# Keys loaded by partition quadrant, values in 8 KB runs, a ring of cells and a third held value pass in a two-layer decode kernel

## The chip, the cores and the metric

The kernel runs on one core of one Trainium2 chip. The metric is the device time of one execution in microseconds (us). Runs of one kernel agree within about 0.5% before the change and within about 1% after it.

## The reference

Two rounds of attention and feed-forward for eight sequences, one new token each. The same caches serve both rounds.

```python
def _A_ref(x, k_cache, v_cache, wq, wo):          # caches: 8 sequences x 8 heads x 8192 rows x 128, bf16
    q = (x @ wq).reshape(B, Sq, Hq, Dh).transpose(0, 2, 1, 3)        # 32 query heads, 4 per cache head
    scores = einsum("bhqd,bhkd->bhqk", q, repeat(k_cache)) * Dh ** -0.5
    o = einsum("bhqk,bhkd->bhqd", softmax(scores), repeat(v_cache))
    return o.transpose(0, 2, 1, 3).reshape(B, Sq, Hq * Dh) @ wo
x = x + _A_ref(layernorm(x), K, V, wq, wo);  x = x + silu_ffn(layernorm(x), w1, w2)
x = x + _A_ref(layernorm(x), K, V, wq, wo);  x = x + silu_ffn(layernorm(x), w1, w2)
```

One head of one sequence has 2 MiB of keys and 2 MiB of values. The kernel reads the keys once (134 MB) and keeps them transposed on the chip between the rounds; it reads the values twice (268 MB). With the weights that makes 482 MB.

## The kernel before

A small planner simulates the kernel when it is built: each load and each computation is a node with an estimated duration. The simulation decides the order in which instructions are written to the queues. Loads go in order through one queue (SP) into a ring of 11 buffers of 512 KB, and a load is issued when a buffer comes free. The parts that the change touches, shortened:

```python
N_GRAN = 11; N_DEF = 2; T_TURN = 1.2              # buffers; value passes held back; planned us of a transpose

def load_v(b, g, P):                              # 4 loads of 512 KB: 128 partitions x 4 KB
    src = A_v_cache[b, g].rearrange("(P n r) d -> P n (r d)", P=4, n=128)
    return load_gran(f"v{b}.{g}.{P}", src[P], 1)

def load_k(b, g, c4):                             # 4 loads of 512 KB: 128 partitions x 4 KB
    src = A_k_cache[b, g].rearrange("(p c4 cg) d -> c4 p (cg d)", p=128, c4=4)
    return load_gran(f"k{b}.{g}.{c4}", src[c4], 1)
# ... (cut)
def turns(b, g):                                  # 32 x 32 blocks of 4-byte words, written 4 words apart
    new = slot(g).bitcast(U32).rearrange("p (k i c4) -> p c4 k i", i=32, c4=4)
    for c4 in range(4):
        kn = load_k(b, g, c4)
        def turn(kn=kn, c4=c4):
            raw = gran(kn.give).bitcast(U32).rearrange("p (k j) -> p k j", j=32)
            op(dve, lambda: dve.transpose(new[:, c4], raw), reads=[res("ring", kn.give)], writes=[res("kt", g)], add=(c4 > 0))
# ... (cut) score matmuls read 128 neighbouring words of the transposed keys as weights; column n of the
# scores becomes partition n of the values, so the row order of keys and values must match
for b in range(-1, NB):                           # sequence b's second round beside b+1's first
    if b >= 0:
        n = ffn_nodes(f"c{b}", prio, b, 1, [x2_node(b, prio)])
        ready = norm_nodes(f"c{b}.ln2", prio, b, 1, [n])
        for h in held:                            # value passes of the sequence before, held back
            values(h)                             # so that the loads go on while ready is computed
    # ... (cut)
            if g % 4 == 0:                        # query weights, 4 x 512 KB into the ring
                second_q.update(queries(f"c{b}", count[0] - 3, g // 4, b, 1, [ready]))
```

Of the kernel before, what the change touches and what calls it, by code (L numbers as in the profile page):

```python
# [11 lines left out]
N_GRAN = 11  # L12
N_SC = 3
N_P = 3
N_DEF = 2
N_OT = 2
N_BD = 4
T_TURN = 1.2
# [94 lines left out]
class Node:  # L113


    __slots__ = ("eng", "dur", "emit", "prio", "deps", "outs", "left", "ready", "end", "take", "give", "name")

    def __init__(self, name, eng, dur, emit, prio, deps):
# [11 lines left out]
        self.give = None  # L130


class Plan:
# [3 lines left out]
    RATE = 2.47  # L137
# [12 lines left out]
    def load(self, name, mib, emit, pool, deps=()):  # L150
        n = Node(name, "DMA", mib * self.RATE, emit, 0, deps)
        n.take = pool
        self.nodes.append(n)
        self.loads.append(n)
        return n

    def run(self, pools):
# [5 lines left out]
        free = {}  # L163
# [10 lines left out]
        waiting = {p: list(b) for p, b in pools.items()}  # L174
# [5 lines left out]
        while True:  # L180
            moved = True
            while moved:
                moved = False
                if li < len(loads):
                    n = loads[li]
                    if n.left == 0 and (n.take is None or waiting[n.take]):
                        buf = waiting[n.take].pop(0) if n.take is not None else None
                        if n.take is not None:
                            n.give = buf
# [23 lines left out]
            elif what == "done":  # L213
                done += 1
                n.end = now
                if n.eng != "DMA" and n.give is not None:
                    for pool, src in n.give:
                        waiting[pool].append(src.give)
# [16 lines left out]
def _build(ctx, nc, A_x, A_k_cache, A_v_cache, A_wq, A_wo, B_w1, B_w2, out):  # L235
# [21 lines left out]
    ring = sb([128, N_GRAN * GR], BF16, "ring")  # L257
# [34 lines left out]
    rsem = [DmaCounter(syn.new_sem(f"ring{i}")) for i in range(N_GRAN)]  # L292
# [16 lines left out]
    def dma(eng, out_ap, in_ap, counter, reads=(), writes=()):  # L309
        syn.acquire(eng, reads, writes)  # L310
        tok = counter.next_tok()
        eng.dma_start(out_ap, in_ap).then_inc(counter.sem, 16)  # L312
        syn.release(tok, reads, writes)

# [13 lines left out]
    def gran(i):  # L328
        return ring[:, i * GR:(i + 1) * GR]
# [8 lines left out]
    def load_gran(name, src, k):  # L338

        n = plan.load(name, 0.5, None, "ring")  # L340

        def emit():
            i = n.give
            dst = gran(i) if k == 1 else gran(i).rearrange("p (k x) -> p k x", k=k)
            dma(sp, dst, src, rsem[i], writes=[res("ring", i)])
# [4 lines left out]
    def load_v(b, g, P):  # L350
        return load_gran(f"v{b}.{g}.{P}", v_src(b, g)[P], 1)

    def v_src(b, g):
        return A_v_cache[b, g].rearrange("(P n r) d -> P n (r d)", P=4, n=128)

    def load_k(b, g, c4):
        src = A_k_cache[b, g].rearrange("(p c4 cg) d -> c4 p (cg d)", p=128, c4=4)
        return load_gran(f"k{b}.{g}.{c4}", src[c4], 1)

    def load_wq(half, kt):  # L360
        return load_gran(f"wq{half}.{kt}", wq_v[:, kt, GR * half:GR * (half + 1)], 1)

    def load_wo(g):
        return load_gran(f"wo{g}", A_wo.rearrange("(g p j) d -> g p (j d)", g=G, j=R)[g], 1)

    def frees(n, pool, src):
        n.give = (n.give or []) + [(pool, src)]
# [7 lines left out]
    def norm_nodes(tag, prio, b0, nb, deps):  # L375
# [54 lines left out]
        m = plan.add(f"{tag}.mean", "DVE", 0.12, mean, prio, [a])  # L430
        v = plan.add(f"{tag}.var", "DVE", 0.3, vari, prio, [m])
        r = plan.add(f"{tag}.root", "POOL", 0.6, root, prio, [v])
        return plan.add(f"{tag}.xn", "DVE", 0.15, apply, prio, [r])


    def ffn_nodes(tag, prio, b0, nb, deps):
# [40 lines left out]
        u = plan.add(f"{tag}.up", "PE", 2.2, up, prio, [n] + ffn_deps)  # L477
        t = plan.add(f"{tag}.tanh", "ACT", 0.3, tanh, prio, [u])
        g = plan.add(f"{tag}.gate", "DVE", 0.15, gate, prio, [t])
        d = plan.add(f"{tag}.down", "PE", 2.2, down, prio, [g])  # L480
        return plan.add(f"{tag}.resid", "DVE", 0.15, resid, prio, [d])


    xr = gran(N_GRAN - 1)[0:NB, 0:D]
    xnr = gran(N_GRAN - 1)[0:NB, D:2 * D]
# [489 lines left out]
```

## Time and profile before

| | before |
|---|---|
| time | 1243.9 us (1242.73 to 1243.91, 3 runs) |
| moved | 484.8 MB, 389 GB/s on average, 408 GB/s on the plateau |
| busy | DVE 57%, PE 51%, the loads' queue 98.7% |

These are lines of the page of the kernel before. The long row has the GB/s of each fortieth of the span. The row of a queue gives packets, MB and the share of the 16 engines' span. A row of part 5 gives the line, engine, operation, output and input, count, busy us and mean ns, and the idle time before it with its releaser. The last two give the count, the KB of a load and its us from issue to landing.

```profile
PE 631.6 (51%) x20640; PEld 593.0 (48%) x20640; DVE 708.4 (57%) x1236; ACT 63.0 (5%) x202; POOL 117.0 (9%) x295
...
GB/s 362 407 398 408 337 371 408 408 408 356 393 408 408 407 371 407 407 408 399 376 409 407 407 394 373 408 408 408 371 389 408 407 407 364 410 407 408 394 339 208
DMA packets 136865, 484.80 MB, mean 389 GB/s; under 512 B 14544, under 2 KB 20448, under 8 KB 136672
...
q1 hardware_dynamic: 136672, 481.90, 98.7%
...
DMA 41%; DVE 25%; issue 20%; PE 10%; SPq 2%; POOL 2%; ACT 0%; POOLq 0%; DVEq 0%
DMA ring<-in_A_k_cache_dram 24%; DVE kts L605 19%; DMA ring<-in_A_v_cache_dram 10%; DMA ring<-in_A_wq_dram 7%; PE sc L656 5%; PE ot L733 2%; SPq L312 2%; DVE sc L678 2%; DVE small L668 2%; PE misc L563 1%; POOL small L673 1%; DVE small L687 1%; POOL small L692 1%; DVE bd L640 0%; PE yt L784 0%
...
L605 DVE STREAM_TRANSPOSE kts<-ring 128x1024 uint32<-128x1024 uint32 x256 | 503.2, 1988 | 116.6 <-DMA ring<-in_A_k_cache_dram 116.4
...
ring<-in_A_v_cache_dram SPq DMA_DIRECT2D x512, 512.0 KB, 10.8
ring<-in_A_k_cache_dram SPq DMA_DIRECT2D x256, 512.0 KB, 10.6
```

The plateau of 408 GB/s fills most slices, and every few slices there is one at 337 to 376: once for each sequence. DVE and PE are busy for half of the time, so the loads bound the kernel. The dips are where compute holds the loads up. The table of windows over one of them shows the columns time, busy us and count of each engine, granted clock, share of the DMA engines, and GB/s:

```profile
core 0: us, PE busy (x) PEld busy (x) DVE busy (x) ACT busy (x) POOL busy (x), PEclk, DMA share, GB/s
270.00:280.00 10.00, 5.06 (x173) 4.76 (x170) 1.44 (x8) 0.18 (x1) 0.56 (x1) 1.00 1.02 406
...
290.00:300.00 10.00, 7.36 (x253) 6.96 (x250) 6.83 (x11) 0.38 (x1) 1.07 (x3) 1.00 0.92 340
300.00:310.00 10.00, 2.70 (x84) 2.47 (x84) 6.18 (x13) 0.77 (x2) 1.34 (x4) 1.00 0.98 380
310.00:320.00 10.00, 6.51 (x229) 6.37 (x230) 5.72 (x10) 0.56 (x2) 0.80 (x2) 1.00 0.94 338
320.00:330.00 10.00, 3.08 (x89) 2.67 (x86) 7.87 (x8) 0.56 (x2) 0.80 (x2) 1.00 1.02 408
```

The waits of the load queue from 270 to 345 us, as engine and line, what was waited for, total us, times, longest us:

```profile
SPq L89 <- DVE kts L605: 19.1, 6, 7.3
SPq L89 <- PE misc L563: 11.2, 2, 6.0
```

The queue waited there for buffers whose keys were not yet transposed and for buffers with query weights.

### The profile page before, as it was taken

The page shows a single profiled execution, that of the slowest core. Times are in us where ns is not written, and L with a number is a line of the kernel's source. Part 1 is how long each engine was busy: PE and PEld are TensorE (multiplying, and loading weights), DVE is VectorE, ACT ScalarE, POOL GpSimd, SP SyncE. Part 2 cuts the span into 40 slices and gives each one's busy share as a digit, 9 for nine tenths or more (in the row PEclk, how much of TensorE's full clock was granted, in tenths as well). Part 3 has the DMA queues.
Part 4 walks back from the last instruction along what each step waited for, and adds up shares of the span by engine and source line. Part 5 has one row for each costly group of instructions (what it writes and reads, how often), then busy time and mean ns, then how long its engine had stood idle before and what let it go on. Part 6 is the DMA issues. An engine that isn't in the chain of part 4 may idle for free.

```text
span 1245.3 us, 45478 instructions
## 1 busy us (share of the span) xinstructions
PE 631.6 (51%) x20640; PEld 593.0 (48%) x20640; DVE 708.4 (57%) x1236; ACT 63.0 (5%) x202; POOL 117.0 (9%) x295
## 2 busy tenths in 40 slices
PE   2334545455554654546454554555555455454555
PEld 2333545445543544545444454544545455444554
DVE  7745466826477265764557546574556826577221
ACT  0000000000000000000000000000000000000000
POOL 1000010101010010110000100110101101011010
DMA  9999999999999999999999999999999999999995
GB/s 362 407 398 408 337 371 408 408 408 356 393 408 408 407 371 407 407 408 399 376 409 407 407 394 373 408 408 408 371 389 408 407 407 364 410 407 408 394 339 208
DMA packets 136865, 484.80 MB, mean 389 GB/s; under 512 B 14544, under 2 KB 20448, under 8 KB 136672
## 3 DMA queue, kind: packets, MB, share of 16 engines
q1 hardware_dynamic: 136672, 481.90, 98.7%
q8 instruction: 162, 2.65, 0.9%
q14 instruction: 31, 0.25, 0.1%
HBM read 481.83 MB, written 0.01 MB: 387 GB/s over the span
## 4 chain that ended last, share of the span: by engine, by line
DMA 41%; DVE 25%; issue 20%; PE 10%; SPq 2%; POOL 2%; ACT 0%; POOLq 0%; DVEq 0%
DMA ring<-in_A_k_cache_dram 24%; DVE kts L605 19%; DMA ring<-in_A_v_cache_dram 10%; DMA ring<-in_A_wq_dram 7%; PE sc L656 5%; PE ot L733 2%; SPq L312 2%; DVE sc L678 2%; DVE small L668 2%; PE misc L563 1%; POOL small L673 1%; DVE small L687 1%; POOL small L692 1%; DVE bd L640 0%; PE yt L784 0%
## 5 line engine op out<-in xcount | busy, mean ns | idle before, releaser
L605 DVE STREAM_TRANSPOSE kts<-ring 128x1024 uint32<-128x1024 uint32 x256 | 503.2, 1988 | 116.6 <-DMA ring<-in_A_k_cache_dram 116.4
L733 PE MATMUL ot<-p,ring 128*128 128x4 bf16 x8192 | 287.4, 167 | 177.0 <-DMA ring<-in_A_v_cache_dram 115.7
L656 PE MATMUL sc<-bd,kts 128*128 128x16 bf16 x8192 | 278.2, 174 | 160.7 <-issue 53.2
L733 PEld LDWEIGHTS ot<-p,ring 128*128 128x128 bf16 x8192 | 255.5, 104 | 193.6 <-DMA ring<-in_A_v_cache_dram 131.1
L656 PEld LDWEIGHTS sc<-bd,kts 128*128 128x128 bf16 x8192 | 249.8, 104 | 168.9 <-issue 56.0
L673 POOL PARTITION_ALL_REDUCE small<-small x128 | 48.1, 376 | 728.9 <-DVE small L668 631.8
L668 DVE TENSOR_REDUCE small<-sc 128x4 f32<-128x256 f32 x128 | 51.9, 406 | 107.6 <-PE sc L656 107.4
L683 ACT ACTIVATE p<-sc 128x256 bf16<-128x256 f32 x128 | 49.0, 383 | 729.6 <-DVE sc L678 729.6
L784 PE MATMUL yt<-z,ring 128*128 128x4 bf16 x1024 | 36.8, 166 | 93.1 <-DVE z L762 89.8
L692 POOL PARTITION_ALL_REDUCE small<-small x128 | 55.0, 431 | 268.4 <-DVE small L687 266.1
L784 PEld LDWEIGHTS yt<-z,ring 128*128 128x128 bf16 x1024 | 33.0, 104 | 96.2 <-issue 96.0
L563 PE MATMUL misc<-xn,ring 128*128 128x1 bf16 (+1 forms) x1152 | 36.2, 166 | 68.7 <-DMA ring<-in_A_wq_dram 62.1
L563 PEld LDWEIGHTS misc<-xn,ring 128*128 128x128 bf16 x1152 | 33.8, 104 | 71.1 <-issue 64.9
L678 DVE TENSOR_TENSOR sc<-sc,small 128x256 f32<-128x256 f32 x128 | 57.1, 447 | 18.2 <-POOL small L673 17.9
L687 DVE TENSOR_REDUCE small<-p 128x4 f32<-128x256 bf16 x128 | 51.2, 401 | 21.3 <-ACT p L683 21.0
L632 PE MATMUL qx<-qab,sel 128*128 128x4 bf16 x256 | 16.6, 169 | 54.5 <-DVE bd L640 54.5
L696 DVE RECIPROCAL small<-small 128x4 f32<-128x4 f32 x128 | 21.6, 168 | 34.6 <-POOL small L692 34.6
L632 PEld LDWEIGHTS qx<-qab,sel 128*128 128x128 bf16 x256 | 11.8, 106 | 56.5 <-DVE bd L640 56.5
L640 DVE TENSOR_TENSOR bd<-qx,mask 128x64 bf16<-128x64 f32 x128 | 27.7, 217 | 16.2 <-PE qx L632 16.0
L571 DVE CAST qtb<-misc 128x4 bf16<-128x4 f32 (+1 forms) x32 | 5.3, 166 | 54.3 <-PE misc L563 54.3
L743 DVE TENSOR_TENSOR qab<-ot,small 128x4 bf16<-128x4 f32 x64 | 10.0, 157 | 43.6 <-PE ot L733 43.4
L762 DVE TENSOR_TENSOR z<-ot,small 128x16 bf16<-128x16 f32 x64 | 10.5, 164 | 37.7 <-PE ot L755 37.7
(61 smaller groups left out, 206.3 us busy)
## 6 DMA issues: line engine op xcount, KB each, us to landing
ring<-in_A_v_cache_dram SPq DMA_DIRECT2D x512, 512.0 KB, 10.8
ring<-in_A_k_cache_dram SPq DMA_DIRECT2D x256, 512.0 KB, 10.6
ring<-in_A_wq_dram SPq DMA_DIRECT2D x72, 512.0 KB, 10.8
ring<-in_A_wo_dram SPq DMA_DIRECT2D x64, 512.0 KB, 11.0
kts<-in_A_wo_dram SPq DMA_DIRECT2D x2, 2048.0 KB, 16.9
w<-in_B_w_dram SPq DMA_DIRECT2D x2, 1792.0 KB, 14.9
ring<-in_A_x_dram SPq DMA_DIRECT2D x1, 8.0 KB
out_dram<-ring SPq DMA_DIRECT2D x1, 8.0 KB
```

The source lines that it names most:

```text
L563: steps.append(lambda h=h, kt=kt, c=c: pe.matmul(qp[:, h * nb:(h + 1) * nb], gran(wn[kt].give)[:, c:c + DH], xn[:, b0:b0 + nb, kt], start= ...
L605: op(dve, lambda: dve.transpose(new[:, c4], raw), reads=[res("ring", kn.give)], writes=[res("kt", g)], add=(c4 > 0))
L632: steps.append(lambda fe=fe: pe.matmul(QX[:, R * fe:R * fe + R], sel[:, fe].rearrange("p a j -> p (a j)"), qsrc, start=True, stop=True))
L656: steps.append(lambda cg=cg, fe=fe: pe.matmul(sc[:, 16 * cg:16 * cg + 16], kv[:, cg, fe // 2, fe % 2], bd[:, 16 * fe:16 * fe + 16], start= ...
L668: op(dve, lambda: dve.tensor_reduce(mxp[sm], sv.rearrange("p (k h) -> p h k", h=R), AX.X, ALU.max), reads=[res(*scr)], writes=[res("mxp", ...
L673: op(pool, lambda: pool.partition_all_reduce(mxa[sm], mxp[sm], 128, bass.bass_isa.ReduceOp.max), reads=[res("mxp", sm)], writes=[res("mxa" ...
L678: op(dve, lambda: dve.tensor_tensor(v, v, mxa[sm].unsqueeze(1).to_broadcast([128, NCH, R]), ALU.subtract), reads=[res("mxa", sm)], writes= ...
L683: op(act, lambda: act.activation(pt[:, :], sv, ACT.Exp, scale=SM_SCALE), reads=[res(*scr)], writes=[res("p", sm)])
L687: op(dve, lambda: dve.tensor_reduce(ssm[sm], pt[:, :].rearrange("p (k h) -> p h k", h=R), AX.X, ALU.add), reads=[res("p", sm)], writes=[re ...
L692: op(pool, lambda: pool.partition_all_reduce(ssa[sm], ssm[sm], 128, bass.bass_isa.ReduceOp.add), reads=[res("ssm", sm)], writes=[res("ssa" ...
L733: steps.append(lambda cg=cg, k=k: pe.matmul(ot[:, 0:R], vt[:, cg, :], pt[:, k:k + R], start=(P == 0 and cg == 0), stop=(P == 3 and cg == N ...
L784: steps.append(lambda j=j, dt=dt: pe.matmul(YT[:, dt * R:(dt + 1) * R], w[:, j, dt * 128:(dt + 1) * 128], zt[:, R * j:R * j + R], start=(g ...
```

## The change

The intent: a transpose that writes neighbouring words should be faster than one that writes a word every 16 bytes. For that the 128 columns of a score block must be (c4, i) instead of (i, c4), and then a value row order exists in which each partition reads 8 KB in one run. The price is that the keys' partitions, (quadrant, i), no longer lie at one stride in the cache. So each 1 MiB half of a head's keys is loaded by four transfers, one for each quadrant of 32 partitions. The ring is cut into cells of 512 KB and keys and values take two neighbouring ones. Three value passes instead of two are held back, and the first query weights come behind the first of them. The planner's durations are revised.

```diff
-N_GRAN = 11
+N_CELL = 11
-N_DEF = 2
+N_DEF = 3
-T_TURN = 1.2
+T_TURN = 1.07
@@ planner: loads take 1 or 2 neighbouring cells (cut) @@
+    def load_cells(name, cells, parts):
+        n = plan.load(name, cells, None)
+        def emit():
+            buf = gran(n.give, cells)
+            for k, (dst, src) in enumerate(parts):
+                dma(sp, dst(buf), src, rsem[n.give], writes=cells_of(n) if k == 0 else (),
+                    adds=cells_of(n) if k else ())
@@ values and keys @@
+    def load_v(b, g, half):
+        src = A_v_cache[b, g].rearrange("(n hh y) d -> hh n (y d)", n=128, hh=2)
+        return load_cells(f"v{b}.{g}.{half}", 2, [(lambda buf: buf, src[half])])
+    def load_k(b, g, half):
+        src = A_k_cache[b, g].rearrange("(c4 i P x) d -> P i c4 (x d)", c4=4, i=32, P=4)
+        return load_cells(f"k{b}.{g}.{half}", 2, [
+            (lambda buf, P=P: buf[32 * P:32 * P + 32, :].rearrange("p (c4 x) -> p c4 x", c4=2),
+             src[P, :, 2 * half:2 * half + 2, :]) for P in range(4)])
@@ transposes @@
-        new = slot(g).bitcast(U32).rearrange("p (k i c4) -> p c4 k i", i=32, c4=4)
+        new = slot(g).bitcast(U32).rearrange("p (k c4 i) -> p c4 k i", i=32, c4=4)
@@ held passes @@
-            for h in held:
+            for k, h in enumerate(held):
+                if k == 1:
+                    second_q.update(queries(f"c{b}", prio, 0, b, 1, [ready]))
                 values(h)
-                    if g % 4 == 0:
+                    if g % 4 == 0 and g >= (4 if held else 0):
@@ revised planner durations of matmuls and small operations (cut) @@
```

More of the change, by code (lines that the diff above doesn't have):

```diff
@@ L113 @@
 class Node:
-    __slots__ = ("eng", "dur", "emit", "prio", "deps", "outs", "left", "ready", "end", "take", "give", "name")
+    __slots__ = ("eng", "dur", "emit", "prio", "deps", "outs", "left", "ready", "end", "take", "give", "name", "cells")
     def __init__(self, name, eng, dur, emit, prio, deps):
@@ L130, in __init__ @@
         self.give = None
+        self.cells = 0
 class Plan:
-    RATE = 2.47
+    RATE = {1: 2.57, 2: 2.51}
     LAND = 2.0
@@ L148, in add, with load @@
         return n
-    def load(self, name, mib, emit, pool, deps=()):
-        n = Node(name, "DMA", mib * self.RATE, emit, 0, deps)
-        n.take = pool
+    def load(self, name, cells, emit, deps=(), ring=True):
+        n = Node(name, "DMA", cells * 0.5 * self.RATE.get(cells, 2.57), emit, 0, deps)
+        n.take = ring
+        n.cells = cells
         self.nodes.append(n)
@@ L155, in load, with place, run @@
         return n
-    def run(self, pools):
+    @staticmethod
+    def place(free, cells):
+        if cells == 1:
+            alone = [c for c in free if c - 1 not in free and c + 1 not in free]
+            return min(alone or free, default=None)
+        starts = [c for c in free if c + 1 in free]
+        return min(starts, default=None)
+    def run(self, cells):
         for n in self.nodes:
@@ L173, in run @@
         wire = 0.0
-        waiting = {p: list(b) for p, b in pools.items()}
+        idle = set(cells)
         for n in self.nodes:
@@ L185, in run @@
                     n = loads[li]
-                    if n.left == 0 and (n.take is None or waiting[n.take]):
-                        buf = waiting[n.take].pop(0) if n.take is not None else None
-                        if n.take is not None:
-                            n.give = buf
+                    at = self.place(idle, n.cells) if n.take else None
+                    if n.left == 0 and (at is not None or not n.take):
+                        if n.take:
+                            n.give = at
+                            idle -= set(range(at, at + n.cells))
                         order.append((now, seq, n))
@@ L216, in run @@
                 if n.eng != "DMA" and n.give is not None:
-                    for pool, src in n.give:
-                        waiting[pool].append(src.give)
+                    for src in n.give:
+                        idle |= set(range(src.give, src.give + src.cells))
                 for o in n.outs:
@@ L255, in bank @@
         return ctx.enter_context(nc.psum_tensor(name, [128, 512], FP32))
-    ring = sb([128, N_GRAN * GR], BF16, "ring")
+    ring = sb([128, N_CELL * GR], BF16, "ring")
     kts = sb([128, G * SLOT], BF16, "kts")
@@ L291, in _build @@
     ksem = [DmaCounter(syn.new_sem(f"kt{i}")) for i in range(2)]
-    rsem = [DmaCounter(syn.new_sem(f"ring{i}")) for i in range(N_GRAN)]
+    rsem = [DmaCounter(syn.new_sem(f"ring{i}")) for i in range(N_CELL)]
     wsem = {n: DmaCounter(syn.new_sem(f"w_{n}")) for n in ("w1", "w2", "x")}
@@ L307, in op, with dma @@
         syn.release(tok, reads, writes, add=add)
-    def dma(eng, out_ap, in_ap, counter, reads=(), writes=()):
+    def dma(eng, out_ap, in_ap, counter, reads=(), writes=(), adds=()):
         syn.acquire(eng, reads, writes)
@@ L313, in dma @@
         syn.release(tok, reads, writes)
+        syn.release(tok, (), adds)
     def mms(steps, reads=(), writes=(), add=False):
@@ L326, in _build, with gran, cells_of @@
     wo_v = A_wo.rearrange("(h p) d -> p h d", p=128)
-    def gran(i):
-        return ring[:, i * GR:(i + 1) * GR]
+    def gran(i, cells=1):
+        return ring[:, i * GR:(i + cells) * GR]
+    def cells_of(n):
+        return [res("ring", n.give + k) for k in range(n.cells)]
     def slot(i, n=1):
@@ L335, in _build, with frees @@
     scored = {}
-    def load_gran(name, src, k):
-        n = plan.load(name, 0.5, None, "ring")
+    def load_cells(name, cells, parts):
+        n = plan.load(name, cells, None)
         def emit():
-            i = n.give
-            dst = gran(i) if k == 1 else gran(i).rearrange("p (k x) -> p k x", k=k)
-            dma(sp, dst, src, rsem[i], writes=[res("ring", i)])
+            buf = gran(n.give, cells)
+            for k, (dst, src) in enumerate(parts):
+                dma(sp, dst(buf), src, rsem[n.give], writes=cells_of(n) if k == 0 else (),
+                    adds=cells_of(n) if k else ())
         n.emit = emit
         return n
-    def load_v(b, g, P):
-        return load_gran(f"v{b}.{g}.{P}", v_src(b, g)[P], 1)
-    def v_src(b, g):
-        return A_v_cache[b, g].rearrange("(P n r) d -> P n (r d)", P=4, n=128)
-    def load_k(b, g, c4):
-        src = A_k_cache[b, g].rearrange("(p c4 cg) d -> c4 p (cg d)", p=128, c4=4)
-        return load_gran(f"k{b}.{g}.{c4}", src[c4], 1)
+    def load_v(b, g, half):
[6 more added lines that the diff above has]
+             src[P, :, 2 * half:2 * half + 2, :]) for P in range(4)])
     def load_wq(half, kt):
-        return load_gran(f"wq{half}.{kt}", wq_v[:, kt, GR * half:GR * (half + 1)], 1)
+        return load_cells(f"wq{half}.{kt}", 1, [(lambda buf: buf, wq_v[:, kt, GR * half:GR * (half + 1)])])
     def load_wo(g):
-        return load_gran(f"wo{g}", A_wo.rearrange("(g p j) d -> g p (j d)", g=G, j=R)[g], 1)
-    def frees(n, pool, src):
-        n.give = (n.give or []) + [(pool, src)]
+        return load_cells(f"wo{g}", 1, [
+            (lambda buf: buf, A_wo.rearrange("(g p j) d -> g p (j d)", g=G, j=R)[g])])
+    def frees(n, src):
+        n.give = (n.give or []) + [src]
     tail = gran(1)
@@ L429, in norm_nodes @@
         a = plan.add(f"{tag}.stats", "PE", 0.3 + 0.2 * nb, stats, prio, deps)
-        m = plan.add(f"{tag}.mean", "DVE", 0.12, mean, prio, [a])
-        v = plan.add(f"{tag}.var", "DVE", 0.3, vari, prio, [m])
+        m = plan.add(f"{tag}.mean", "DVE", 0.18, mean, prio, [a])
+        v = plan.add(f"{tag}.var", "DVE", 0.45, vari, prio, [m])
         r = plan.add(f"{tag}.root", "POOL", 0.6, root, prio, [v])
-        return plan.add(f"{tag}.xn", "DVE", 0.15, apply, prio, [r])
+        return plan.add(f"{tag}.xn", "DVE", 0.3, apply, prio, [r])
     def ffn_nodes(tag, prio, b0, nb, deps):
@@ L476, in ffn_nodes @@
         n = norm_nodes(tag + ".ln", prio, b0, nb, deps)
-        u = plan.add(f"{tag}.up", "PE", 2.2, up, prio, [n] + ffn_deps)
-        t = plan.add(f"{tag}.tanh", "ACT", 0.3, tanh, prio, [u])
-        g = plan.add(f"{tag}.gate", "DVE", 0.15, gate, prio, [t])
-        d = plan.add(f"{tag}.down", "PE", 2.2, down, prio, [g])
-        return plan.add(f"{tag}.resid", "DVE", 0.15, resid, prio, [d])
-    xr = gran(N_GRAN - 1)[0:NB, 0:D]
-    xnr = gran(N_GRAN - 1)[0:NB, D:2 * D]
+        u = plan.add(f"{tag}.up", "PE", 1.65, up, prio, [n] + ffn_deps)
+        t = plan.add(f"{tag}.tanh", "ACT", 0.2, tanh, prio, [u])
+        g = plan.add(f"{tag}.gate", "DVE", 0.18, gate, prio, [t])
+        d = plan.add(f"{tag}.down", "PE", 1.65, down, prio, [g])
+        return plan.add(f"{tag}.resid", "DVE", 0.18, resid, prio, [d])
+    xr = gran(N_CELL - 1)[0:NB, 0:D]
+    xnr = gran(N_CELL - 1)[0:NB, D:2 * D]
     st6 = negm[0:NB, 0:6]
     mv = var[0:NB, 0:2]
-    last = res("ring", N_GRAN - 1)
+    last = res("ring", N_CELL - 1)
     def consts():
@@ L508, in _build @@
     c_n = plan.add("consts", "POOL", 1.5, consts, -10)
-    x_n = plan.load("x", 0.05, lambda: dma(sp, xr, x_in, wsem["x"], writes=[last]), None)
+    x_n = plan.load("x", 1, lambda: dma(sp, xr, x_in, wsem["x"], writes=[last]), ring=False)
     def first_norm():
@@ L545, in _build @@
     f5 = plan.add("f.copy", "DVE", 0.4, first_copy, -5, [f4])
-    frees(f4, "ring", x_n)
-    x_n.give = N_GRAN - 1
+    frees(f4, x_n)
+    x_n.give = N_CELL - 1
     def queries(tag, prio, half, b0, nb, deps):
@@ L565, in mul @@
                             start=(kt == 0), stop=(kt == KT - 1)))
-                mms(steps, reads=[res("ring", w.give) for w in wn] + [res("xn")], writes=[res("misc")])
+                mms(steps, reads=[r for w in wn for r in cells_of(w)] + [res("xn")], writes=[res("misc")])
             def copy(g0=g0, g1=g1, qp=qp):
@@ L575, in copy @@
                        reads=[res("misc")], writes=[res("qab", g) for g in range(g0, g1)])
-            m = plan.add(f"{tag}.q{g0}", "PE", 0.65 * (g1 - g0), mul, prio, wn + deps + last)
+            m = plan.add(f"{tag}.q{g0}", "PE", 0.5 * (g1 - g0), mul, prio, wn + deps + last)
             last = [plan.add(f"{tag}.qc{g0}", "DVE", 0.17, copy, prio, [m])]
@@ L581, in queries @@
         for w in wn:
-            frees(m, "ring", w)
+            frees(m, w)
         return out_n
@@ L598, in turns, with turn @@
         tn = []
-        new = slot(g).bitcast(U32).rearrange("p (k i c4) -> p c4 k i", i=32, c4=4)
-        for c4 in range(4):
-            kn = load_k(b, g, c4)
-            def turn(kn=kn, c4=c4):
-                raw = gran(kn.give).bitcast(U32).rearrange("p (k j) -> p k j", j=32)
-                op(dve, lambda: dve.transpose(new[:, c4], raw), reads=[res("ring", kn.give)],
-                   writes=[res("kt", g)], add=(c4 > 0))
-            n = plan.add(f"t{b}.{g}.{c4}", "DVE", T_TURN, turn, count[0] + 0.5, [kn] + scored.get(g, []) + tn[-1:])
-            frees(n, "ring", kn)
-            tn.append(n)
+        new = slot(g).bitcast(U32).rearrange("p (k c4 i) -> p c4 k i", i=32, c4=4)
+        for half in range(2):
+            kn = load_k(b, g, half)
+            for c in range(2):
+                def turn(kn=kn, c=c, c4=2 * half + c):
+                    raw = gran(kn.give, 2).bitcast(U32).rearrange("p (c k j) -> p c k j", c=2, j=32)
+                    op(dve, lambda: dve.transpose(new[:, c4], raw[:, c]), reads=cells_of(kn),
+                       writes=[res("kt", g)], add=(c4 > 0))
+                tn.append(plan.add(f"t{b}.{g}.{2 * half + c}", "DVE", T_TURN, turn, count[0] + 0.5,
+                                   [kn] + scored.get(g, []) + tn[-1:]))
+            frees(tn[-1], kn)
         kept[b, g] = tn
@@ L659, in score @@
                 mms(steps, reads=[res("kt", g), res("bd", u % N_BD)], writes=[res(*scr)], add=(q > 0))
-            sn.append(plan.add(f"s{u}.{q}", "PE", 0.75, score, pr - 1,
+            sn.append(plan.add(f"s{u}.{q}", "PE", 0.56, score, pr - 1,
                                [tn[3], bn] + ([old[1]] if old else []) + sn[-1:]))
@@ L723, in values @@
         for P in range(4):
-            if P == 3 and wo is not None:
+            if P == 2 and wo is not None:
                 h["wo"] = load_wo(wo)
-            vn = load_v(b, g, P)
+            if P % 2 == 0:
+                vn = load_v(b, g, P // 2)
             def pv(P=P, vn=vn):
-                vt = gran(vn.give).rearrange("p (cg d) -> p cg d", cg=NCG)
+                vt = gran(vn.give, 2).rearrange("p (a cg d) -> p a cg d", a=2, cg=NCG)[:, P % 2]
                 steps = []
@@ L735, in pv @@
                         start=(P == 0 and cg == 0), stop=(P == 3 and cg == NCG - 1)))
-                mms(steps, reads=[res("ring", vn.give), res("p", sm)], writes=[res("ot", o)], add=(P > 0))
-            n = plan.add(f"v{u}.{P}", "PE", 0.65, pv, pr, [h["exp"], vn, old] + vs[-1:])
-            frees(n, "ring", vn)
+                mms(steps, reads=cells_of(vn) + [res("p", sm)], writes=[res("ot", o)], add=(P > 0))
+            n = plan.add(f"v{u}.{P}", "PE", 0.56, pv, pr, [h["exp"], vn, old] + vs[-1:])
+            if P % 2:
+                frees(n, vn)
             vs.append(n)
@@ L787, in mul @@
                         skip_group_check=True))
-            mms(steps, reads=[res("ring", wn.give), res("z", o)], writes=[res("yt")], add=g > 0)
-        n = plan.add(f"w{h['u']}", "PE", 0.65, mul, count[0] - 3, [h["n"], wn, prev])
-        frees(n, "ring", wn)
+            mms(steps, reads=cells_of(wn) + [res("z", o)], writes=[res("yt")], add=g > 0)
+        n = plan.add(f"w{h['u']}", "PE", 0.56, mul, count[0] - 3, [h["n"], wn, prev])
+        frees(n, wn)
         return n
@@ L808, in mul @@
                 writes=[res("yt")], add=g > 0)
-        return plan.add(f"e.w{g}", "PE", 0.65, mul, count[0] - 3, [h["n"], wn, prev])
+        return plan.add(f"e.w{g}", "PE", 0.56, mul, count[0] - 3, [h["n"], wn, prev])
     free_yt = [None]
@@ L821, in load_ffn @@
     def load_ffn():
-        ffn_deps.append(plan.load("w1", 1.75, lambda: dma(
-            sp, w1_sb[:, :, :], B_w1.rearrange("(kt p) f -> p kt f", p=128), wsem["w1"], writes=[res("w1")]), None))
-        ffn_deps.append(plan.load("w2", 1.75, lambda: dma(
-            sp, w2_sb[:, :, :], B_w2.rearrange("(ft p) d -> p ft d", p=128), wsem["w2"], writes=[res("w2")]), None))
+        ffn_deps.append(plan.load("w1", 3.5, lambda: dma(
+            sp, w1_sb[:, :, :], B_w1.rearrange("(kt p) f -> p kt f", p=128), wsem["w1"], writes=[res("w1")]), ring=False))
+        ffn_deps.append(plan.load("w2", 3.5, lambda: dma(
+            sp, w2_sb[:, :, :], B_w2.rearrange("(ft p) d -> p ft d", p=128), wsem["w2"], writes=[res("w2")]), ring=False))
     def x2_node(b, prio):
@@ L838, in load_wo_all @@
         for i in range(2):
-            n = plan.load(f"woall{i}", 2.0, None, None, scored[2 * i])
+            n = plan.load(f"woall{i}", 4, None, scored[2 * i], ring=False)
             def emit(i=i):
@@ L934, in _build @@
     n = plan.add("e.copy", "DVE", 0.5, e_copy, big, [n])
-    order = plan.run({"ring": list(range(N_GRAN - 1))})
+    order = plan.run(range(N_CELL - 1))
     with nc.Block() as block:
```

## The prediction

> **What bounds the kernel now.** Loading. The page counts 484.8 MB in 1245.3 us (389 GB/s), while DVE is busy 57% and PE 51%. The 40 slices show a plateau of 408 GB/s: at that rate the bytes alone take 484.8/408 = 1188 us. The other 57 us are slices below the plateau: about 4 us at the start, about 21 us in the last two slices (the last 15 us move 12 GB/s), and about 32 us in one dip per batch. In a table of 10 us windows the first dip (130 to 170 us) runs at 263, 338, 358, 341 GB/s, the next (280 to 320 us) at 363, 340, 380, 338. There the DMA queue waits for buffers: the queue's own waits there name transposes (19.1 us) and query projections (11.2 us). DVE works through 1.99 us transposes that delay the softmax and normalization steps behind which the held values and query weights sit.
>
> **What changes, costed.**
> 1. Transposes: 256 x 1988 ns (groups by line), for 1024 elements written at a 16-byte stride. [...] DVE is not the bound, so this pays only by shortening the dips.
> 2. Values: 512 loads of 512 KB become 256 of 1 MiB in 8 KB runs. Two rates of this trace give the price of a packet: while the second feed-forward weight lands (1 KB runs) 350 GB/s, that is 46.8 ns per packet and engine; 4 KB runs at 408, 160.6 ns. A line through both (an estimate) gives 8 KB in 312 ns, or 419 GB/s: 268 MB gain about 17 us. This is on the bound.
> 3. A third held pass, and the first query weights loaded after the first held pass: 5 us more of loads that need no result of the feed-forward chain. With point 1, I expect 15 to 22 of the 32 us of dips to go.
> 4. Ring: the same 11 cells, but 1 MiB units are freed later; costs a few us.
> 5. Keys: 256 loads over 128 partitions become 512 of 256 KB over 32 partitions each. Issues on SP cost 0.45 us (timeline, first four), so 1.8 us per MiB against 2.6 us of transfer: hidden.
>
> **Main risk.** [...] Nothing in this trace tests it: every large load there spans 128 partitions. The rest of the change only makes sense if the keys keep their rate, so I hold this less likely than not, at about one in four.
>
> **Predicted:** 1207 us (-3%), range 1180 to 1290. Faster by over 2%: 0.63; within 2%: 0.13; slower: 0.24.
>
> **What would show it.** [...] packets down by some 32,000; slices of values alone at 415 to 420 GB/s; dips once per batch shallower, above 380 GB/s; start and tail as before; windows with key loads as fast as those with values. If wrong: [...] the plateau stays at 408 (then about 1222 us); or dips remain because 1 MiB cells come free too late.

The forecast's sum stands at 1207 us: 1243.9 us before, less about 17 (point 2) and 15 to 22 (point 3), plus a few (point 4). The terms of the main risk said how slow the keys would be if a transfer to 32 partitions were slower than one to 128. They made a second sum, some 1490 us in all. Nothing measured stood behind them then; m1 below measures the rate.

## The result, and the profile after

The changed kernel takes 1686.26 us (1674.02 to 1690.83, 4 runs) against 1243.91 us in the same rounds: 1.354 times as long, 95% interval 1.347 to 1.362. A ratio here is the mean time of one kernel's fast runs over that of the other's of the same rounds, so it is not quite the ratio of the medians quoted beside it.

The lines of the page after that answer to those above:

```profile
PE 630.1 (37%) x20640; PEld 591.2 (35%) x20640; DVE 548.0 (32%) x1236; ACT 62.2 (4%) x202; POOL 117.4 (7%) x295
...
GB/s 258 302 296 268 239 316 275 253 333 304 310 248 231 319 294 313 252 230 321 321 314 279 253 309 312 301 260 302 340 301 278 247 325 290 288 262 239 303 368 242
DMA packets 104094, 484.78 MB, mean 287 GB/s; under 512 B 14544, under 2 KB 20448, under 8 KB 71136
...
q1 hardware_dynamic: 103904, 481.90, 95.4%
...
DMA 71%; issue 9%; DVE 7%; PE 7%; SPq 5%; POOL 1%; ACT 0%; POOLq 0%; DVEq 0%
DMA ring<-in_A_k_cache_dram 36%; DMA ring<-in_A_v_cache_dram 33%; DVE kts L626 5%; SPq L326 5%; PE ot L755 3%; DMA ring<-in_A_wq_dram 1%; PE sc L677 1%; PE misc L584 1%; PE misc L468 1%; PE misc L486 1%; POOL rstd L434 0%; POOL small L694 0%; DVE sc L699 0%; PE yt L807 0%; DVE small L689 0%
...
L626 DVE STREAM_TRANSPOSE kts<-ring 128x1024 uint32<-128x1024 uint32 x256 | 310.8, 1230 | 252.1 <-DMA ring<-in_A_k_cache_dram 252.0
...
ring<-in_A_v_cache_dram SPq DMA_DIRECT2D x256, 1024.0 KB, 15.2
ring<-in_A_k_cache_dram SPq DMA_DIRECT2D x512, 256.0 KB, 10.3
```

The bytes are the same, but the average fell from 389 to 287 GB/s and no slice reaches even 370. The queue's packets still fill 95.4% of the engines' time. The transposes fell from 1988 to 1230 ns and DVE's busy time from 708 to 548 us, and the packets from 136,865 to 104,094, as the change intended. In the chain that ended last, loads rose from 41% to 71% and DVE fell from 25% to 7%. The table of windows near the start, with the columns as above, shows two rates:

```profile
4.00:6.00 2.00, 0.37 (x8) 0.29 (x8) 0.40 (x1) 0.00 (x0) 0.78 (x4) 1.00 1.04 229
6.00:8.00 2.00, 0.00 (x0) 0.00 (x0) 0.00 (x0) 0.00 (x0) 0.00 (x0) 1.00 1.06 229
8.00:10.00 2.00, 0.00 (x0) 0.00 (x0) 1.60 (x4) 0.00 (x0) 0.00 (x0) 1.00 1.01 215
...
14.00:16.00 2.00, 0.00 (x0) 0.00 (x0) 1.46 (x2) 0.00 (x0) 0.00 (x0) 1.00 0.99 395
...
18.00:20.00 2.00, 0.85 (x26) 0.80 (x27) 0.19 (x1) 0.00 (x0) 0.00 (x0) 1.00 1.06 221
```

From 4 to 10 us only keys are under way, and 215 to 229 GB/s arrive at a full DMA share. At 14 us the query weights have their turn, over 128 partitions, and 395 arrive; at 18 us keys again, and 221. (The first packet of values starts at 26 us.)

### The profile page after: what moved, and what is told of

Same layout as the page of the kernel before. It is cut to its first block, busy times and chain, and to the rows that moved or that the text cites. A ratio compares the mean times of both kernels' runs of the same rounds, so it can differ in the third digit from the quotient of the medians.

```text
span 1686.8 us, 44976 instructions
## 1 busy us (share of the span) xinstructions
PE 630.1 (37%) x20640; PEld 591.2 (35%) x20640; DVE 548.0 (32%) x1236; ACT 62.2 (4%) x202; POOL 117.4 (7%) x295
## 2 busy tenths in 40 slices
DMA packets 104094, 484.78 MB, mean 287 GB/s; under 512 B 14544, under 2 KB 20448, under 8 KB 71136
## 3 DMA queue, kind: packets, MB, share of 16 engines
q1 hardware_dynamic: 103904, 481.90, 95.4%
## 4 chain that ended last, share of the span: by engine, by line
DMA 71%; issue 9%; DVE 7%; PE 7%; SPq 5%; POOL 1%; ACT 0%; POOLq 0%; DVEq 0%
DMA ring<-in_A_k_cache_dram 36%; DMA ring<-in_A_v_cache_dram 33%; DVE kts L626 5%; SPq L326 5%; PE ot L755 3%; DMA ring<-in_A_wq_dram 1%; PE sc L677 1%; PE misc L584 1%; PE misc L468 1%; PE misc L486 1%; POOL rstd L434 0%; POOL small L694 0%; DVE sc L699 0%; PE yt L807 0%; DVE small L689 0%
## 5 line engine op out<-in xcount | busy, mean ns | idle before, releaser
L626 DVE STREAM_TRANSPOSE kts<-ring 128x1024 uint32<-128x1024 uint32 x256 | 310.8, 1230 | 252.1 <-DMA ring<-in_A_k_cache_dram 252.0
L677 PE MATMUL sc<-bd,kts 128*128 128x16 bf16 x8192 | 274.7, 174 | 254.9 <-DVE kts L626 223.4
L766 DVE TENSOR_TENSOR qab<-ot,small 128x4 bf16<-128x4 f32 x64 | 10.1, 158 | 88.5 <-PE ot L755 88.4
L653 PE MATMUL qx<-qtb,sel 128*128 128x4 bf16 x256 | 16.6, 168 | 33.8 <-DVE bd L661 32.4
L653 PEld LDWEIGHTS qx<-qtb,sel 128*128 128x128 bf16 x256 | 11.9, 105 | 37.1 <-DVE bd L661 33.2
L653 PE MATMUL qx<-qab,sel 128*128 128x4 bf16 x256 | 16.6, 168 | 21.7 <-DVE bd L661 16.3
```

The lines of the kernel that those rows point to most:

```text
L626: op(dve, lambda: dve.transpose(new[:, c4], raw[:, c]), reads=cells_of(kn), writes=[res("kt", g)], add=(c4 > 0))
L677: steps.append(lambda cg=cg, fe=fe: pe.matmul(sc[:, 16 * cg:16 * cg + 16], kv[:, cg, fe // 2, fe % 2], bd[:, 16 * fe:16 * fe + 16], start= ...
```

## The experiments

Rival theories at the start. **A (partitions):** which partitions a transfer touches sets its rate, so the keys by quadrant run at about half rate (215 to 229 GB/s against 395 for the weights over 128 partitions, in the windows above). **B (small transfers):** 512 transfers of 256 KB instead of 256 of 512 KB cost the time. **C (ring):** cells of 1 MiB come free too late, or the third held pass starves the queue. The expectations also gave a reason for A, a mechanism that no run here shows. What A forecast by that reason alone stands as the author's guess beside what was measured.

One caution holds for every run below that is called correct: four kernels that pair keys with the wrong value rows (e1, e1b, e2, e6) passed the comparison with the reference. I take it that the softmax is nearly flat for these inputs (argued, not tested). So that comparison does not vouch for a row order; where a layout matters I say which one it is.

### m1: the shapes alone

Eight phases of key loads with no compute, drained between phases; the output is wrong.

```python
phases = [("wide 8 KB", wide(4096)), ("wide 4 KB", wide(2048)), ("four wide 2 KB", four_wide),
          ("quadrants 0 1 2 3", quads((0, 1, 2, 3))), ("quadrants 0 2 1 3", quads((0, 2, 1, 3))),
          ("partitions 0 to 63", half(0)), ("partitions 32 to 95", half(32)),
          ("quadrants, two queues", quads((0, 2, 1, 3), act))]
```

> Loads alone, no compute; the output is wrong on purpose. Eight phases of 8 MiB from the key cache, each drained before the next: (1) 128 partitions x 8 KB, (2) 128 x 2 runs of 4 KB, (3) four loads of 256 KB over 128 partitions in 2 KB runs, (4) quadrants 0 1 2 3, four loads of 256 KB over 32 partitions, as in the changed kernel, (5) the same in the order 0 2 1 3, (6) 4 MiB over partitions 0 to 63, (7) 4 MiB over partitions 32 to 95, (8) quadrants with every other load from the ACT queue. Theory A [...]: 1 about 419 GB/s, 2 about 408, 3 about 385, 4 about 222, 5 about 222 or somewhat more, 6 about 222, 7 about 408, 8 above 300. Rival B (a load of 256 KB, or one of few partitions, is slow as such): 3 also near 222 and 7 no better than 6.

One window inside each of the eight phases, in that order; the last two columns are the DMA share and GB/s (before them stand the length, an idle engine and the clock):

```profile
core 0: us, POOL busy (x), PEclk, DMA share, GB/s
5.00:20.00 15.00, 0.00 (x0) 1.00 1.02 427
28.00:44.00 16.00, 0.00 (x0) 1.00 1.03 413
55.00:69.00 14.00, 0.00 (x0) 1.00 1.05 390
75.00:107.00 32.00, 0.00 (x0) 1.00 1.04 223
116.00:146.00 30.00, 0.00 (x0) 1.00 1.04 236
152.00:168.00 16.00, 0.00 (x0) 1.00 1.04 206
178.00:182.00 4.00, 0.00 (x0) 1.00 1.02 382
192.00:212.00 20.00, 0.00 (x0) 1.00 1.04 300
```

The quadrants run at 223 GB/s against 413 for the same 4 KB runs over 128 partitions. Small transfers as such are not slow: 256 KB over 128 partitions run at 390. What decides is which partitions: 64 of them starting at 0 get 206 GB/s, 64 starting at 32 get 382, though that phase is so short (4 MiB) that its window is 4 us. The order 0 2 1 3 shows 236 against 223, which is 6% more, and quadrants split over two queues reach 300. B falls. Why the partitions matter is not shown; theory A holds here as these measured rates.

### e1: wide keys in the changed kernel

```diff
-        src = A_k_cache[b, g].rearrange("(c4 i P x) d -> P i c4 (x d)", c4=4, i=32, P=4)
-        return load_cells(f"k{b}.{g}.{half}", 2, [
-            (lambda buf, P=P: buf[32 * P:32 * P + 32, :].rearrange("p (c4 x) -> p c4 x", c4=2),
-             src[P, :, 2 * half:2 * half + 2, :]) for P in range(4)])
+        src = A_k_cache[b, g].rearrange("(c4 p x) d -> p c4 (x d)", c4=4, p=128)
+        return load_cells(f"k{b}.{g}.{half}", 2, [
+            (lambda buf: buf.rearrange("p (c4 x) -> p c4 x", c4=2), src[:, 2 * half:2 * half + 2, :])])
```

> The changed kernel, with each key half loaded by one transfer over 128 partitions, still 2 runs of 4 KB in each partition, so the same bytes and packets; keys land in other partitions, so the output is wrong on purpose. Everything else of the change stays: unit stride, 8 KB value runs, cells, three held passes. Theory A [...]: the keys run at 408 GB/s again, about 1205 us. Rival C (the ring of 1 MiB units or the third held pass starves the queue): above 1500 us.

Measured: 1221.07 us (4 runs) against 1243.29; ratio 0.982 (0.980 to 0.984). The row order is wrong, so this is no replacement for the kernel. From its page:

```profile
GB/s 364 413 401 415 300 415 413 414 390 416 413 409 414 390 416 411 401 416 395 406 395 416 416 390 413 399 413 394 414 415 412 414 392 416 411 407 416 380 384 201
...
q1 hardware_dynamic: 97760, 481.87, 97.9%
...
L625 DVE STREAM_TRANSPOSE kts<-ring 128x1024 uint32<-128x1024 uint32 x256 | 308.9, 1226 | 36.7 <-DMA ring<-in_A_k_cache_dram 36.2
```

With 128 partitions the loss is gone, and everything else of the change is still in place. So the key loads carry all of it, and C falls. The plateau is now 413 to 416 GB/s, and a slice is still near 390 once for each sequence.

### e2: as many small transfers, but wide

```diff
+        src = A_k_cache[b, g].rearrange("(c4 p h x) d -> p c4 h (x d)", c4=4, p=128, h=2)
+        return load_cells(f"k{b}.{g}.{half}", 2, [
+            (lambda buf, q=q: buf[:, 1024 * q:1024 * q + 1024], src[:, 2 * half + q // 2, q % 2, :])
+            for q in range(4)])
```

> The changed kernel, with each key half loaded by four transfers of 256 KB, as in it, but each over 128 partitions with 2 KB runs; wrong output on purpose. As many transfers and issues as the changed kernel. Theory A [...]: about 1225 us (2 KB packets near 387 GB/s by the line through the packet prices). Rival B (four small transfers per half cost the time): near 1680 us.

Measured: 1243.99 us in one run (wrong row order). Theory A's 1225 was too low by 19 us, but B's 1680 is far off: the number and size of the transfers cost 23 us against e1 at most, and part of that is the price of 2 KB runs.

### e3 and e4: the quadrants in another order, and on two queues

Both keep the layout of the changed kernel. e3 issues the quadrants as 0 2 1 3; e4 does so and issues every other one, which is 2 and 3, from the ACT queue.

```diff
-             src[P, :, 2 * half:2 * half + 2, :]) for P in range(4)])
+             src[P, :, 2 * half:2 * half + 2, :]) for P in (0, 2, 1, 3)])
@@ e4 only (shortened) @@
+            for q in (sp, act)[:len(parts)]:
+                syn.acquire(q, writes=cells_of(n))
-                dma(sp, dst(buf), src, rsem[n.give], ...)
+                dma(act if k % 2 else sp, dst(buf), src, rsem[n.give])
```

> The changed kernel with the quadrants issued in the order 0 2 1 3[...]; output correct. Theory A in its strict form [...]: within 3% of 1686 us. [...] Rivals B and C: no change.

> The changed kernel with quadrants 0 and 1 issued from SP and 2 and 3 from ACT[...]; output in the right layout. With loads alone this shape ran at about 302 GB/s against 222. Theory A [...]: keys near 300 GB/s, so 134 MB x (1/222 - 1/302) = 160 us less and less harm to the values: 1400 to 1500 us. Rivals B and C: no change, near 1686 us.

Measured: e3 1568.06 us, e4 1615.71 us, one run each. Both are faster than the 1686 us of the changed kernel, as m1's loads were in the same shapes (236 and 300 GB/s against 223). But e3 gains 118 us, more than its faster keys can give: 134 MB x (1/223 - 1/236) = 33 us. It missed the range that stands (within 3% of 1686 us, the author's guess). It lies in the second one, 1400 to 1600, which rested on the unshown mechanism alone. e4 missed its range (1400 to 1500): in loads alone that shape ran at 300 GB/s against 236 for the same order on one queue, but in the kernel it came out slower than e3, so there the second queue gained nothing; why is open. Its 8 KB value packets took 388 ns on average in the trace's packet records, against 317 in e1.

### l1: the loads of the changed kernel with no compute

The half rate of the keys (223 against 413 GB/s in m1) explains only part. Keys at 222 GB/s instead of 408 are 134 MB x (1/222 - 1/408) = 276 us; the change lost 442. So I took all computation out of the changed kernel. A cell is then free as soon as it has landed. (The last store now waits for every load.)

```diff
     def op(eng, inst_fn, reads=(), writes=(), add=False):
-        syn.acquire(eng, reads, () if add else writes)
-        ...
+        return
     def mms(steps, reads=(), writes=(), add=False):
-        syn.acquire(pe, reads, writes, own=False)
-        ...
+        return
```

> The loads of the changed kernel in its order and its cells, with every computation left out, so that a cell is free as soon as it has landed; output wrong on purpose. If a load slows only itself: 134 MB at 222, 268 MB at 420 and 82 MB at about 400 make 605 + 639 + 205 = 1449 us and some 10 us of ends. If keys still on the way slow the values behind them (the 8 KB packets of the changed kernel took 380 ns on average against 317 with wide keys): 1550 to 1620 us, with such packets again. If the other 200 us come from waits on compute: near 1460 us.

Measured: 1680.64 us in one run, as long as the whole changed kernel and longer than all three forecasts. The rest of the loss is therefore in the load stream itself and needs no compute. From its page:

```profile
GB/s 261 318 315 334 325 320 304 380 300 306 244 244 351 294 271 229 227 362 275 271 245 224 327 274 265 265 224 283 325 259 250 247 298 338 259 251 240 251 398 331
...
q1 hardware_dynamic: 103904, 481.90, 96.7%
```

In the packet records the 8 KB value packets took 378 ns on average. The values are slower, though nothing about them is narrow.

### m2: do keys slow the values behind them?

```python
phases = [("kkvvvv" * 3, quads, False), ("k" * 6 + "v" * 12, quads, False),   # values: 128 x 8 KB
          ("kkvvvv" * 3, quads, True), ("kkvvvv" * 3, wide_k, False)]         # True: drained at each change
```

> Loads alone again, output wrong on purpose: four phases of 18 MiB (6 MiB of keys, 12 MiB of values), drained between phases. (1) Keys by quadrant and values in turns of 2 and 4 MiB, as in the changed kernel, nothing waits; (2) the same bytes, all keys first, then all values; (3) as 1, but every change from keys to values or back waits until all has landed; (4) as 1 with keys over 128 partitions. If a key load slows only itself: 1 and 2 both take 28 us (keys at 222) + 30 us (values at 426) = 58 us, 3 some 10 us more for five waits, 4 about 45 us. If keys still on the way slow the values behind them: 1 is longer than 2 by 5 us or more, and in 3 the 8 KB packets take 310 ns throughout.

Measured, from the start of the first packet to the end of the last: 59.8 us for phase 1 (from 1.7 to 61.5), 59.2 for 2, 70.7 for 3 and 46.1 for 4. So turns cost nothing over three turns: in phase 1 the values ran at 419 to 423 GB/s and the keys near 222. The theory that every key load slows the values behind it falls: in phase 1 only 4% of the packets of values have one of keys under way beside them.

### m3, l2, l3, e7: do the engines drift apart?

What differed was length. In l1 most slices of the first quarter run at 300 to 335 GB/s, and most later ones at 225 to 300. The completion increments of the ring's semaphores, taken in groups of 16 over all loads, lay 0.9 us apart (median) in the first tenth of l1 and 5.5 us or more in each of the last seven. So theory S, an inference: the 16 DMA engines that share a transfer (the trace has 16 completion increments of each) drift apart, and values on some of them slow down while others are still on keys. m3 runs 24 turns of 2 MiB of keys by quadrant and 4 MiB of values through a ring of 5 cells of 1 MiB, then through 16 cells, then through 5 with a wait for everything before each turn.

> Loads alone, output wrong on purpose: three phases of 24 turns, each turn 2 MiB of keys by quadrant and 4 MiB of values. (1) A ring of 5 cells of 1 MiB, about as deep as in the changed kernel; (2) a ring of 16 cells; (3) 5 cells, and before each turn a wait for all that is under way. In step a turn takes 9.4 + 9.9 = 19.3 us, so 463 us for 24 turns. Theory S (engines drift apart [...]): 1 starts near 19.5 us a turn and gets slower, to 22 us or more; 3 stays flat near 22 us (19.3 plus one drain and restart) with values at full rate. If a shallow ring alone is the cause: 1 is slow from its first turns, 2 is 19.3 us a turn, and 3 is no better than 1. If neither: 1 and 2 both near 463 us.

The timeline of the load queue gives the start of each turn's keys in us, the time to issue them and their count. Two turns early in phase 1, two in its middle, two near its end, and four of phase 3:

```profile
32.26 4.17 SPq L68 DMA_DIRECT2D buf<-in_A_k_cache_dram  x8
52.06 4.16 SPq L68 DMA_DIRECT2D buf<-in_A_k_cache_dram  x8
...
308.42 4.19 SPq L68 DMA_DIRECT2D buf<-in_A_k_cache_dram  x8
328.10 4.20 SPq L68 DMA_DIRECT2D buf<-in_A_k_cache_dram  x8
...
416.80 3.94 SPq L68 DMA_DIRECT2D buf<-in_A_k_cache_dram  x8
440.13 3.97 SPq L68 DMA_DIRECT2D buf<-in_A_k_cache_dram  x8
...
1025.10 3.62 SPq L68 DMA_DIRECT2D buf<-in_A_k_cache_dram  x8
1046.83 3.61 SPq L68 DMA_DIRECT2D buf<-in_A_k_cache_dram  x8
...
1458.86 3.62 SPq L68 DMA_DIRECT2D buf<-in_A_k_cache_dram  x8
1480.60 3.61 SPq L68 DMA_DIRECT2D buf<-in_A_k_cache_dram  x8
```

A turn takes 19.8 us early (52.06 - 32.26) and 19.7 still at the eighteenth; then it lengthens to 23.3 (440.13 - 416.80). In phase 3 it stays at 21.7 from the first to the last. Phase 2, with the deeper ring, went from 19.8 to 20.4 us a turn. So the shallow ring is not slow as such; the slowdown builds up, and a wait before each turn prevents it.

The packet records show what changes. They give each packet's start, time and size, but not its engine. In phase 1, 4% of the value packets of the first 100 us have a packet of keys under way at their midpoint, and the mean value packet takes 327 ns; from 400 to 490 us it is 62%, and 428 ns. In phase 3 it is 2%, and 326 ns. The same count in the whole kernels, where packets of 4 KB are keys or weights:

| 8 KB value packets | beside a 4 KB packet | mean of these, ns | mean of the others, ns |
|---|---|---|---|
| changed kernel | 62% | 408 | 336 |
| e1, wide keys | 52% | 315 | 319 |
| e7, waits added (below) | 26% | 356 | 323 |

So keys and values under way together do no harm when both span 128 partitions (315 against 319 ns); with keys by quadrant the values beside them are slow (408 against 336 ns).

l2 is l1 with the wide keys of e1, the control:

> The loads alone of the wide-key form, the same order and cells; control for the loads alone of the changed kernel. [...] 1160 to 1185 us (484.8 MB at 416 GB/s). If the order, the cells or the values of 1 MiB have a fault of their own: above 1250 us.

```profile
GB/s 365 415 401 416 417 415 415 417 418 417 415 416 416 417 419 414 415 419 417 416 415 415 417 419 417 414 415 418 418 415 416 416 419 417 416 414 417 418 413 328
```

1170.29 us, as forecast: order, cells and 1 MiB values have no fault of their own, and with wide keys the completion spread did no harm (1.5 us in the median, rising from 0.35 to 2.8). The spread by itself is not the fault: it was about 3 us (median) in the kernel before and in the changed kernel alike. l3 and e7 add one wait to l1 and to the whole changed kernel, before the first quadrant of each of the 64 key units (shortened):

```diff
+            if align:                              # first half of a head's keys
+                for c in rsem:
+                    if c.val and syn.waited.get((sp.engine, c.sem), 0) < c.val:
+                        sp.wait_ge(c.sem, c.val)
```

> The loads alone of the changed kernel, with one wait for everything under way before each of the 64 key units, so that the 16 engines start level. It only adds waits. Theory S: the waits cost 64 x about 2.5 us = 160 us and save the 230: 1580 to 1640 us, faster than 1679, with 8 KB packets near 320 ns. Otherwise: 1780 us or more.

> The changed kernel, whole and with correct layout, with the same wait before each key unit. Theory S: 1600 to 1690 us, and 8 KB packets near 320 ns against 380. Otherwise: above 1750 us.

Measured: l3 1588.78 us, 92 us less than l1 by adding nothing but waits; its 8 KB packets took 327 ns on average. e7 1687.31 us, no gain over 1686: its value packets fell to 332 ns, but its queue is busy for only 88.5% of the span, against 95.4%, so the waits cost what the faster packets saved. It lies inside its forecast (1600 to 1690), whose upper end meant no gain. One run each. The queue's line of e7:

```profile
q1 hardware_dynamic: 103904, 481.90, 88.5%
```

### e1b, e6: the other parts of the change, with wide keys

e1b is e1 with `N_DEF = 2`; e6 is e1 with values in 128 x 2 runs of 4 KB.

> The wide-key form of the changed kernel with two value passes held back instead of three. If the third held pass carries weight: 5 to 15 us slower than 1221 us. If it does not: within 3 us of it. Wrong key rows as in the wide-key run.

> The wide-key form of the changed kernel with values in 1 MiB loads of 128 partitions x 2 runs of 4 KB instead of one of 8 KB (rows of keys and values do not match, as there). By the packet prices the 8 KB runs are worth 17 us: about 1238 us. If they are worth nothing: 1221 us.

| | time, us (4 runs) | against e1's 1221.07 | ratio to before (95%) |
|---|---|---|---|
| e1b, two held passes | 1230.17 | +9.1 | 0.989 (0.986 to 0.991) |
| e6, 4 KB values | 1236.33 | +15.3 | 0.993 (0.992 to 0.995) |

e1 and these two were timed in different rounds; the kernel before took 1243.3 to 1244.9 in all of them. Both parts are worth about what was forecast.

### g1, g2, g3: versions in a right layout

g1 keeps the old row order and its strided transposes, with keys in 128 x 8 KB, values in 128 x 2 x 4 KB, and the cells, planner and three held passes of the change. g2 is the kernel before with only the third held pass and the earlier query weights. g3 is g2 with `T_TURN = 1.9`.

> A version with the right layout [...]: the old row order with its 16-byte strided transposes, keys in 1 MiB loads of 128 partitions x 8 KB, values in 1 MiB loads of 128 x 2 runs of 4 KB, with the cells and the three held passes of the change. Theory A: keys gain about 8 us by fewer packets (134 MB x (1/408 - 1/420)), the dips some 10 us: 1215 to 1235 us. If the unit stride carried the rest of the gain: 1240 us or more.

> The kernel before, right layout and all its loads of 512 KB, with three held passes and the first query weights behind the first of them. If this part carries its 9 us from the wide-key form over: about 1234 us. If the slow transposes hide it: 1240 to 1245 us.

> As the run before this one, with the planner told that a transpose takes 1.9 us, as measured, instead of 1.2. Order of instructions changes only. If the planned order was misled by the wrong duration: 1220 to 1232 us; if not: within 4 us of the run before.

| | time, us (4 runs) | before in the same rounds | ratio (95%) |
|---|---|---|---|
| g1 | 1299.13 | 1244.23 | 1.044 (1.041 to 1.047) |
| g2 | 1232.43 | 1244.86 | 0.990 (0.989 to 0.992) |
| g3 | 1247.61 | 1244.86 | 1.003 (1.001 to 1.004) |

g1 missed theory A's range by 64 us or more; it lies in the other branch (1240 us or more, the unit stride carrying the gain). Its transposes take 1970 ns again, but its planner counts them at 1.07 us. e6 has the same planner, cells, values and held passes and took 1236.33 us: it differs in the stride (1226 ns) and in key runs of 4 KB. So cells of 1 MiB alone do not explain g1; the slow transposes and their wrong planned time together do, and the two are not separated. g3 shows that the planned duration alone can move the time by 15 us, and that the truer value was the worse one. A version with unit stride, wide keys, wide values and right rows was not found: in wide keys the quadrant bits lie just above the 32 rows of a block, and in wide values the bits c4 must lie there (argued). g2 is the version to use: 1.0% faster than before, its interval clear of 1, in the old row order.

## Why the prediction was wrong

**The step that failed** is point 5 with the weight given to the main risk. The prediction counted the keys as hidden behind their issue cost: "1.8 us per MiB against 2.6 us of transfer". The issue cost was right (8 issues took 3.6 us), but the transfer was not 2.6 us: 1 MiB of keys at 222 GB/s takes 4.7. The risk that loads to 32 partitions are slow was seen and costed (the sum was some 1490 us), and then held unlikely with "The rest of the change only makes sense if the keys keep their rate". That is an argument about the author of the change, not about the chip, and the prediction says itself that nothing in its trace tested it: "every large load there spans 128 partitions".

**A second term was mis-sized.** The risk path came to some 1490 us; 1686 were measured. Some 14 of the missing 200 us are gains that the rest of the change did not bring (e1: 1221 against 1207). Nearly all the others are slow values and idle engines, which the prediction did not have. Packet records of the changed kernel against e1, which differs in the keys alone, divide their difference of 468 us of span:

| term | from | us |
|---|---|---|
| 4 KB packets (keys, query and output weights) | 50,176 x (252.6 - 164.3) ns / 16 engines | 277 |
| 8 KB packets (values) | 32,768 x (380.4 - 316.9) ns / 16 engines | 130 |
| idle engines | (1686.8 x 4.6%) - (1218.7 x 2.1%) | 52 |

Some 9 us remain undivided. The first term is close to the 276 us worked out under l1 for keys at 222 GB/s instead of 408, though it also holds 17,408 packets of weights. I read the second and third as the engines out of step. Shown: the slow values need no compute (l1), are not there in the first turns of loads alone (m2, m3), grow with time there (m3), come where narrow loads are under way beside them (packet records) and mostly go when waits are added (l3: 327 ns a packet against 378 in l1). That one engine's late keys slow another engine's early values is inferred from this; the records do not name the engine, and where the two would meet is not shown. In the changed kernel it is no slow build-up: the value packets of its first tenth already took 379 ns, 76% of them beside a 4 KB packet. If the engines are out of step, what puts them so, there and in m3, is open.

**What held**, as seen in e1 and its variants:

- Bound: loads bound the kernel; removing the fault of the loads removed the loss. No run isolates what DVE's 160 us less of work are worth; g1 against e6 puts them, with g1's wrong plan, at 63 us, so in this plan they are not free.
- Point 1: the direction held. The transposes took 1230 ns at unit stride against 1988 with a word every 16 bytes, and DVE saved 160 us of busy time. What the prediction said of their size rested on no trace.
- Point 2: 8 KB runs are worth 15.3 us (17 forecast); the median value packet of e1 took 312 ns (312 forecast). The median packet took 84 ns for 2 KB (e2), 159 for 4 KB (before) and 309 for 8 KB (m1).
- Point 3: the third held pass is worth 9 us in e1 and, with the earlier query weights, 12 us in g2. But e1 as a whole gained 22 us where the prediction summed to 37. Dips near 390 GB/s remain, and the first one is no shallower (a slice of 300 GB/s against 337 before): the first sequence has no held passes, and the queue's longest wait there, 12.4 us, was for the query projection.
- Point 4: l2 against e1 (1170 and 1221 us) bounds all that compute costs the loads, the ends included, at 51 us.

## What to carry to other kernels

A layout that makes a compute operation faster may narrow the transfer that feeds it: first ask which partitions each single transfer touches, and time that shape alone before building on it (the m1 program took 220 us of chip time). When a risk that no trace tests stands against the guess that the author must have checked, test it first: here the risk was real (223 against 413 GB/s). And a narrow load can cost more than its own bytes: here it slowed the values beside it too (408 against 336 ns a packet).
